# First batch fetched in halves of 48 rows, the sum of f put ahead of its rounded copy, and new offsets for the planner of a spectral and gated feed-forward kernel

## The chip, the core and the metric

The kernel runs on one core of a Trainium2 chip. The metric is the device time of one execution in microseconds (us). TensorE is called PE, VectorE DVE, ScalarE ACT, GpSimd POOL, and SyncE SP, which issues the DMAs; PEld is the load of weights into PE. About 0.2% of the time, 5.1 us, is what a measurement of this kernel can tell from no change.

## The reference, cut to what matters

```python
X = np.fft.rfft(x, axis=1)                      # x: 8 batches, 3008 tokens, 256 channels
Yr = Xr @ w_r - Xi @ w_i + b_r
Yi = Xr @ w_i + Xi @ w_r + b_i
Y  = sign(Y) * max(abs(Y) - 0.01, 0)            # each part by itself
y  = np.fft.irfft(Yr + 1j * Yi, n=3008, axis=1)
t  = y.reshape(24064, 256)
out = (silu(t @ w_gate) * (t @ w_val)) @ w_out  # 256 -> 1536 -> 256
```

## The kernel before, in words

There are two stages. The first, about the first 515 us, is the spectral one: the transform over 3008 = 47 x 64 tokens, the mixing of the channels, the shrinking and the transform back. The second, the remaining 2040 us, is the gated feed-forward part, 24 blocks of tokens by 6 pairs of hidden slices, in an order written out by hand. The change does not touch the second stage.

The first stage is made of named steps:

- `x_first k` (k = 0 to 7, first batch only) fetches 128 rows of 1024 numbers. In the prepared input, rows 0 to 46 and 64 to 110 hold tokens, row 47 and row 111 hold zeros, and the other 32 rows hold zeros that nothing reads: the products take rows 0 to 47 and 64 to 111. A row of this input stands 4352 bytes after the one before.
- `first k` is the product of that chunk with the small constant matrix `wa` (48 x 64 by 48 x 512, function `stage_a`) into two banks of PSUM. Two `turn` steps, transposes on DVE, then carry the banks to SBUF. For the later batches the same is done by `x k` and `tiles k`, each `x k` in one transfer of 128 rows.
- For each of 96 pairs (8 batches by 12): `second` (PE, from the turned chunks and the constants `wf`) writes `ps_b`. ACT copies one half of it to `f` (step `f`) and rounds the whole (step `f_hi`); DVE adds the other half to `f` (step `f_sum`) and takes the rest that rounding lost (`f_lo`); ACT and POOL or DVE do the same for the sum (`flat_hi`, `flat_lo`). `sum` (PE) multiplies the sum, `spread` (DVE) puts it with the bias into `mixb`, `mix` (PE) adds the two other products, and `gather`, `clip`, `shrink`, `y_hi`, `y_lo`, `back`, `z` and `store` follow. `ps_b` is one bank, so `second` of a pair waits for `f_lo` of the pair before.
- `z_in n` fetches, in two transfers of 48 rows each (rows 0 to 47, then rows 64 to 111, 4 KB a row), what `store` wrote to DRAM; two rows of one of these transfers lie 64 KB apart in DRAM.
- `load_seven` turns 18 weight matrices of 64-bit numbers into rounded halves, between the pairs.

The set-up also makes three rounded weight matrices: `wm 1` and `wm 2` (POOL) from `wj` and `wr`, then `wm_hi`, `negate`, `bias` (ACT) and `wm_lo` (POOL).

All steps are handed to a planner (class `Plan`). Each has a key, and the table `SHIFT` moves the keys of a kind of step; the planner simulates the engines with a fixed cost for each step and writes out one order for each engine, and an engine keeps that order. Where the planner sees PE idle in the first 40 us it puts in `idle` products, whose results nothing uses.

Before the planned order, POOL clears the tile `warm`, ACT loads a table with one activation on that tile, and PE multiplies `warm` by itself three times (L719 and L721).

Of the kernel before, what the change touches and what calls it, by code (L numbers as in the profile page):

```python
# [44 lines left out]
FEED = 84  # L45
SHIFT = {"add": -0.5, "lower": 0.5, "third": -0.5, "turn5": 0.12, "turn4": 0.06, "turn0": -0.44, "y_hi": -0.37, "f": -0.5, "out": 0.75, "spread": 0.0, "back": -0.19, "raw": 0.37, "second": 0.06, "y_lo": 0.68, "shrink": 0.44, "z_in": 0.06, "mix": 0.5, "wr": -1.0, "turn1": 0.0, "tiles": 0.56, "turn6": -0.31, "wo": 0.06, "x_sum": -0.5, "sum": -0.5, "flat_lo": -0.12, "xt1": 0.18, "x": 0.12, "store": 0.37, "turn": -0.32, "wm": -0.12, "bits down": -0.5, "upper": 0.25, "wj": -0.12, "kept": -1.0, "negate": 0.25, "turn3": 0.12, "unit": 0.56, "wm_hi": -0.12, "z": 0.5, "bias": -0.44, "wi_lo": -0.06, "turn2": -0.18, "x_hi": -0.5, "clip": -0.5, "xt0": -0.25, "wa": 0.06, "warm": 0.25, "bits up": -1.5}
# [4 lines left out]
WARM = 1  # L51
FULL = 40.0
# [223 lines left out]
def transform(ctx, tc, front, ring, last, ps_, feed, xp, w_r, w_i, cb, wup_raw, wdn_raw, ca, cf, ci, cq, w21, wup_d, wdn_d, xt_d, d2):  # L276
    nc = tc.nc
# [37 lines left out]
    def head(plan):  # L315
# [4 lines left out]
        def fetch_first(k):  # L320
            where = ("x_raw", "x_raw", "wo", "wo", "z_in", "z_in", "z_in", "w")[k]
            if where == "x_raw":
                box[k] = take()
            elif where == "w":
                box[k] = scratch[:, : 2 * T]
            elif where == "z_in":
                box[k] = last.tile([P, 2 * T], F32, name="x_first", tag=where, bufs=3)
            else:
                if k == 2:
                    box["wo"] = last.tile([P, 4 * T], F32, name="x_first", tag=where, bufs=1)  # L330
                box[k] = box["wo"][:, (k - 2) * 2 * T : (k - 1) * 2 * T]
# [800 lines left out]
```

## Time and profile before

| what | us |
|---|---|
| median of 3 runs (2557.44 to 2557.63) | 2557.52 |
| the profiled execution's own time | 2556.73 |
| its span, first to last instruction | 2554.9 |
| PE busy in the span | 2544.8 |
| DVE, POOL and ACT busy | 2064.7, 2082.1 and 1705.0 |

The 1.8 us between the span and the execution's own time lie around the program. "Busy" of PE is modelled, since products are pipelined. The page shows a granted clock of 90% or more in every slice. A row of the timeline has its start, its length, the engine, the line, the operation, and in brackets how long the engine was idle before it and what ended that; a DMA named there has landed just before.

### The profile page before, as it was taken

What the parts mean: (1) busy time and instruction counts of PE and PEld (TensorE: products, weight loads), DVE (VectorE), ACT (ScalarE), POOL (GpSimd) and SP (SyncE); (2) the same over time, 40 slices, a digit from 0 to 9 for tenths busy, and PEclk for the clock granted to TensorE, in tenths of its full rate; (3) what the DMA queues carried; (4) which work ended last, traced back from release to release, by engine and by line L of the source; (5) the groups of instructions that cost most, each with busy time, mean ns of one, the idle gap of its engine ahead of it and who ended that gap; (6) DMA issues with size and microseconds to landing.
All of it is one profiled execution on the core that took longest, in us unless ns stands there. A gap on an engine that the chain in (4) does not pass through costs nothing.

```text
span 2554.9 us, 45902 instructions
## 1 busy us (share of the span) xinstructions
PE 2544.8 (100%) x16534; PEld 2136.0 (84%) x16534; DVE 2064.7 (81%) x2998; ACT 1705.0 (67%) x3342; POOL 2082.1 (81%) x1595
## 2 busy tenths in 40 slices
PE   9999999999999999999999999999999999999999
PEld 6888888978888888888888888888888888888899
DVE  7989898677877877887788788878887888788887
ACT  6888888966666665666656666666666566656665
POOL 5777777568888888888888888888888888888886
PEclk9999999999999999999999999999999999999999
DMA  6788888855445444544444444444444444444453
GB/s 236 246 293 277 287 281 273 252 206 183 159 154 177 163 154 153 175 157 151 160 158 150 141 163 163 151 142 163 163 151 143 162 163 146 142 158 158 151 182 123
DMA packets 133924, 460.57 MB, mean 180 GB/s; under 512 B 13632, under 2 KB 58944, under 8 KB 133696
## 3 DMA queue, kind: packets, MB, share of 16 engines
q1 hardware_dynamic: 133552, 457.53, 54.0%
q8 instruction: 131, 2.15, 0.4%
q14 instruction: 97, 0.79, 0.1%
q10 hardware_dynamic: 144, 0.10, 0.0%
HBM read 366.61 MB, written 90.96 MB: 179 GB/s over the span
## 4 chain that ended last, share of the span: by engine, by line
PE 97%; DVE 1%; DMA 1%; ACT 0%; issue 0%; POOL 0%; SPq 0%; DVEq 0%
PE bank L791 79%; PE mixb L535 5%; PE ps_b L513 3%; PE ps_s L520 3%; PE ps_z L559 3%; PE ps_x L650 2%; PE ps_a L470 2%; PE bank L1037 0%; DMA x_first<-xp 0%; DMA scratch<-xp 0%; PE ps_z L557 0%; DVE y_lo L594 0%; ACT t L547 0%; DVE f_lo L578 0%; POOL t L586 0%
## 5 line engine op out<-in xcount | busy, mean ns | idle before, releaser
L791 PE MATMUL bank<-x_near,wup 128*128 128x512 f32 (+1 forms) x4032 | 1035.8, 386 | 0.4 <-DVE bank L964 0.2
L811 POOL TENSOR_TENSOR h_parts<-more,h_parts 128x512 fp32r<-128x512 f32 (+1 forms) x572 | 847.2, 1495 | 101.8 <-ACT h_parts L807 100.7
L791 PEld LDWEIGHTS bank<-x_near,wup 128*128 128x128 f32 x4032 | 751.0, 188 | 152.7 <-DVE bank L964 3.9
L791 PE MATMUL bank<-h_parts,wdn 128*128 128x512 f32 (+1 forms) x3024 | 835.3, 385 | 0.0
L811 POOL TENSOR_TENSOR h_parts<-hidden,h_parts 128x512 fp32r<-128x512 f32 (+1 forms) x431 | 563.7, 1319 | 213.7 <-ACT h_parts L807 176.9
L791 PEld LDWEIGHTS bank<-h_parts,wdn 128*128 128x128 f32 x3024 | 564.9, 188 | 108.5 <-POOL h_parts L811 0.3
L807 ACT CAST h_parts<-hidden 128x512 fp32r<-128x512 f32 (+1 forms) x433 | 265.5, 613 | 451.0 <-DVE hidden L937 449.7
L791 PE MATMUL bank<-x_parts,wup 128*128 128x512 f32 (+1 forms) x2016 | 525.7, 384 | 0.0
L937 DVE TENSOR_TENSOR hidden<-hidden,bank 128x512 f32<-128x512 f32 (+1 forms) x576 | 375.8, 674 | 78.1 <-PE bank L791 69.6
L791 PEld LDWEIGHTS bank<-x_parts,wup 128*128 128x128 f32 x2016 | 375.4, 188 | 71.7 <-DVE bank L964 1.7
L832 DVE TENSOR_TENSOR sums<-sums,bank 128x512 f32<-128x512 f32 (+1 forms) x357 | 240.2, 673 | 234.3 <-PE bank L791 234.3
L807 ACT CAST h_parts<-more 128x512 fp32r<-128x512 f32 (+1 forms) x572 | 349.3, 611 | 39.3 <-DVE more L802 28.4
L935 ACT ACTIVATE hidden<-bank 128x512 f32<-128x512 f32 (+1 forms) x432 | 252.6, 585 | 114.6 <-PE bank L791 113.9
L802 DVE TENSOR_TENSOR more<-hidden 128x512 f32<-128x512 f32 (+1 forms) x286 | 291.9, 1059 | 0.0
L802 DVE TENSOR_TENSOR more<-hidden,more 128x512 f32<-128x512 f32 (+1 forms) x286 | 257.7, 901 | 0.0
L942 ACT COPY bank<-bank 128x512 f32<-128x512 f32 (+1 forms) x288 | 161.6, 561 | 109.3 <-DVE hidden L937 103.9
L964 DVE TENSOR_TENSOR bank<-hidden,bank 128x512 f32<-128x512 f32 (+1 forms) x288 | 196.9, 684 | 36.3 <-PE bank L791 23.5
L586 POOL TENSOR_TENSOR t<-t,y 128x512 f32<-128x512 f32 x94 | 129.3, 1376 | 70.1 <-DVE y L585 63.1
L950 ACT COPY hidden<-bank 128x512 f32<-128x512 f32 (+1 forms) x288 | 167.6, 582 | 2.2
L547 ACT COPY t<-mixb 64x256 f32<-64x256 f32 x384 | 140.9, 367 | 22.0 <-PE mixb L535 17.1
L243 POOL TENSOR_TENSOR x_near<-xf,x_near 128x512 fp32r<-128x512 f32 (+1 forms) x112 | 142.3, 1286 | 5.2 <-PE bank L791 4.8
L986 DVE TENSOR_TENSOR hidden<-hidden,bank 128x512 f32<-128x512 f32 (+1 forms) x144 | 97.4, 676 | 42.7 <-PE bank L791 42.4
(111 smaller groups left out, 3104.1 us busy)
## 6 DMA issues: line engine op xcount, KB each, us to landing
wup<-wup_d SPq DMA_DIRECT2D x288, 896.0 KB, 4.7
scratch<-xp SPq DMA_DIRECT2D x59, 512.0 KB, 4.9
out<-o SPq DMA_DIRECT2D x88, 256.0 KB, 6.1
d<-z SPq DMA_DIRECT2D x84, 256.0 KB, 3.9
z_in<-d SPq DMA_DIRECT2D x112, 192.0 KB, 5.1
xt_d<-xt SPq DMA_DIRECT2D x56, 376.0 KB, 4.7
xf<-xt_d SPq DMA_DIRECT2D x15, 1024.0 KB, 7.8
wup_d<-wup SPq DMA_DIRECT2D x12, 896.0 KB, 5.8
```

Source lines behind the costliest of these rows:

```text
L243: low = lambda: eng.tensor_tensor(part[:, 1, :h], src, f32(part[:, 0, :h]), op=ALU.subtract)
L547: nc.scalar.copy(t()[64 * half : 64 * half + 64, k * C : (k + 1) * C], mixb[64 * k : 64 * k + 64, half * C : (half + 1) * C])
L791: nc.tensor.matmul(o, lhsT=weights[w], rhs=parts[x], start=start and i == 0, stop=stop and i == 2, skip_group_check=True)
L802: v.tensor_tensor(at(o, h), at(a, h), at(b, h), op=ALU.subtract)
L807: act.copy(pair[i][:, 0, :h], at(i, h))
L811: eng.tensor_tensor(pair[i][:, 1, :h], at(i, h), f32(pair[i][:, 0, :h]), op=ALU.subtract)
L832: v.tensor_tensor(o, o, spare[:, :h], op=ALU.add)
L935: act.activation(at(i, h), src, AF.Silu)
L937: v.tensor_tensor(at(i, h), at(i, h), src, op=ALU.mult)
L942: act.copy(b3[:, :h], b1[:, :h])
L950: act.copy(m5, b2[:, :h])
L964: v.tensor_tensor(b2[:, :h], m5, b3[:, :h], op=ALU.add)
```

## The change

1. `x_first k` becomes two transfers, rows 0 to 47 and rows 64 to 111, and the unread rows are not fetched. SP issues 16 transfers in place of 8.
2. `wa` has no transfer of its own. It stands in 64 more columns of the first chunk; POOL copies it to its place, and `first 0` reads it where it landed.
3. DVE, not POOL, clears `warm`, and the activation that loads the table has a tile of its own, so PE's first products no longer wait for ACT. They are two of 128 columns and one of 512; the second of 512 (`clear`) stands behind `first 7`.
4. `wr` and `wj` change places, and offsets move `wf 0` behind the other constants. `wm 1`, `wm 2` and the `wm_lo` may run on POOL or DVE.
5. After planning, `f_sum` is put ahead of `f_hi` in the program's order, by moving one of the two past steps of other engines, so that `f_sum` is not behind `f_hi` in what it waits for.
6. `SHIFT` has new numbers and 17 more kinds of step, `BIAS` (which engine a step takes) four new ones, and 24 single steps have a `NUDGE`.

```diff
-SHIFT = {"add": -0.5, "lower": 0.5, "third": -0.5, "turn5": 0.12, ...
+SHIFT = {"add": -0.5, "lower": 0.68, "third": -0.5, "turn5": 0.15, ...
-BIAS = {'y_lo POOL': 0.2, 'z DVE': 1.7, 'flat_lo DVE': 1.2, 'shrink DVE': 1.5}
+BIAS = {"y_lo POOL": 0.3, "z DVE": 0.7, "flat_lo DVE": 2.2, "shrink DVE": 0.8}
+NUDGE = {"shrink 33": -0.5, "flat_lo 17": -0.25, "tiles 41": 0.25, ...
-        key += SHIFT.get(name.split()[0], 0) * SLOT
+        key += (SHIFT.get(name.split()[0], 0) + NUDGE.get(name, 0)) * SLOT
+    HALVES = slice(0, 48), slice(64, 112)
-            nc.sync.dma_start(box[k], xp[0, k, :, : 2 * T])
+            wide = 2 * T if k else 2 * T + 64
+            if not k:
+                box[k] = scratch[:, 5 * T : 5 * T + wide]
+            for rows in HALVES:
+                nc.sync.dma_start(box[k][rows], xp[0, k, rows, :wide])
-        plan.add("wa", "SP", 0.45, -39.5, [], load_wa, 2.0)
+        plan.add("wa", "POOL", 0.2, -39.5, ["x_first 0"], lambda: [g.tensor_copy(wa[rows], box[0][rows, 2 * T :]) for rows in HALVES])
-        plan.add("wr", "SP", 0.45, -24, [], load("wr", ...
-        plan.add("wj", "SP", 0.45, -23, [], load("wj", ...
+        plan.add("wr", "SP", 0.45, -19.2, [], load("wr", ...
+        plan.add("wj", "SP", 0.45, -23.8, [], load("wj", ...
+        either = {"POOL": 1.23, "DVE": 0.61}
-        plan.add("wm_lo 0", "POOL", 1.23, 0.3 * SLOT, ["wm_hi 0"], lambda: lower(0))
+        plan.add("wm_lo 0", either, None, 0.3 * SLOT, ["wm_hi 0"], lambda eng: lower(0, eng), wide=True)
...
-    nc.gpsimd.memset(warm, 0.0)
-    nc.scalar.activation(warm[:, 0:1], warm[:, 0:1], AF.Silu)
-    for _ in range(WARM):
-        nc.tensor.matmul(mixed[0][:, :C], lhsT=warm[:, :P], rhs=warm[:, C:], start=True, stop=True)
-    for bank in mixed:
-        nc.tensor.matmul(bank, lhsT=warm[:, :P], rhs=warm, start=True, stop=True)
+    table = k1p.tile([P, 1], F32, name="table")
+    v.memset(warm, 0.0)
+    nc.gpsimd.memset(table, 0.0)
+    nc.scalar.activation(table, table, AF.Silu)
+    for _ in range(2):
+        clear(0, P)
+    clear(0)
+    plan.add("clear", "PE", 0.87, -1.0, ["turn 0 10", "turn 0 11"], lambda: clear(1))
     order = plan.order()
+    for j in range(B * NP):
+        names = [name for name, _ in order]
+        i, k = names.index(f"f_hi {j}"), names.index(f"f_sum {j}")
+        between = {engine for _, engine in order[i + 1 : k]}
+        if i < k and "ACT" not in between:
+            order.insert(k, order.pop(i))
+        elif names.index(f"f {j}") < i < k and "DVE" not in between:
+            order.insert(i, order.pop(k))
```

How the order moves, at three places. The first is SP's queue at the start of the program. Before (`scratch` and `x_first` are the eight chunks, `wa`, `wr`, `wj`, `wf`, `bias` and `raw_i` the constants):

```order
L332 DMA scratch<-xp 128x1024
L309 DMA wa<-ca 128x64
L332 DMA scratch<-xp 128x1024
L332 DMA x_first<-xp 128x1024 x5
L332 DMA scratch<-xp 128x1024
L350 DMA wr<-w_r 128x2x256
L313 DMA wf<-cf 128x768
L350 DMA bias<-bias 128x512
L350 DMA wj<-w_i 128x2x256
L350 DMA raw_i<-ci 128x256
```

And of the change:

```order
L335 DMA scratch<-xp 48x1088 x2
L335 DMA scratch<-xp 48x1024 x2
L335 DMA x_first<-xp 48x1024 x10
L335 DMA scratch<-xp 48x1024 x2
L353 DMA wj<-w_i 128x2x256
L353 DMA wr<-w_r 128x2x256
L353 DMA raw_i<-ci 128x256
L353 DMA bias<-bias 128x512
L312 DMA wf<-cf 128x768
```

The chunks are 16 transfers of 48 rows, `wa` is gone, and `wf` moved from the second of the constants to the last.

The second is ACT's order from its first step on the weights to the first rounded sum (`wm_hi` and `wsum` are the weights, `f` and `f_hi` of pair 0). Before:

```order
L372 CAST wm_hi<-wr 128x512
L383 ACTIVATE bias<-bias 32x256 x2
L576 COPY f<-ps_b 128x256
L575 CAST f_hi<-ps_b 128x4x2x64
L375 CAST wm_hi<-wsum 128x512
L579 CAST f_hi<-f 128x256
L384 CAST wi_hi<-raw_i 128x256
L377 ACTIVATE wsum<-wsum 128x512
L378 CAST wm_hi<-wsum 128x512
```

And of the change:

```order
L377 CAST wm_hi<-wr 128x512
L380 CAST wm_hi<-wsum 128x512
L388 ACTIVATE bias<-bias 32x256
L382 ACTIVATE wsum<-wsum 128x512
L383 CAST wm_hi<-wsum 128x512
L388 ACTIVATE bias<-bias 32x256
L389 CAST wi_hi<-raw_i 128x256
L582 COPY f<-ps_b 128x256
L581 CAST f_hi<-ps_b 128x4x2x64
L585 CAST f_hi<-f 128x256
```

All steps on the weights, the bias and `wi_hi` now stand ahead of the first `f`; before, four of them stood behind it.

The third is PE from its first product to the last of the eight `first` (`mixb` from `warm` are products whose results nothing uses, `ps_a` are the `first`). Before:

```order
L719 MATMUL mixb_130<-warm 128x256
L721 MATMUL mixb_130<-warm 128x512
L721 MATMUL mixb_131<-warm 128x512
L470 MATMUL ps_a<-scratch,wa 64x512 x8
L470 MATMUL ps_a<-x_first,wa 64x512 x20
L470 MATMUL ps_a<-scratch,wa 64x512 x4
```

And of the change:

```order
L727 MATMUL mixb_130<-warm 128x128 x2
L727 MATMUL mixb_130<-warm 128x512
L476 MATMUL ps_a<-scratch 64x512 x4
L476 MATMUL ps_a<-scratch,wa 64x512 x4
L476 MATMUL ps_a<-x_first,wa 64x512 x20
L476 MATMUL ps_a<-scratch,wa 64x512 x4
L727 MATMUL mixb_131<-warm 128x512
```

The products ahead of the first `ps_a` shrink from one of 256 and two of 512 columns to two of 128 and one of 512, and the other of 512 stands behind the last `first`.

## Rows read from the trace of the kernel before

**Rows 1.** The page: busy time of each engine; the chain that ended last.

```profile
PE 2544.8 (100%) x16534; PEld 2136.0 (84%) x16534; DVE 2064.7 (81%) x2998; ACT 1705.0 (67%) x3342; POOL 2082.1 (81%) x1595
...
PE 97%; DVE 1%; DMA 1%; ACT 0%; issue 0%; POOL 0%; SPq 0%; DVEq 0%
```

**Rows 2.** Windows: stretch, length, busy by engine, granted clock, DMA share, GB/s.

```profile
0.00:20.00 20.00, 16.25 (x116) 7.13 (x116) 10.66 (x18) 4.65 (x10) 4.17 (x8) 1.00 0.91 338
...
20.00:100.00 80.00, 78.28 (x587) 64.30 (x580) 70.77 (x124) 64.05 (x152) 55.80 (x53) 1.00 0.63 205
100.00:500.00 400.00, 399.76 (x6031) 351.52 (x6029) 342.88 (x562) 343.72 (x814) 306.06 (x276) 1.00 0.88 280
```

**Rows 3.** Timeline of PE in the first 26 us: start, length, work.

```profile
2.28 1.22 PE L719 MATMUL mixb<-warm 128*128 128x256 f32 x2 [2.28 <-ACT warm L717]
3.29 3.22 PE L721 MATMUL mixb<-warm 128*128 128x512 f32 x4
6.45 1.95 PE L470 MATMUL ps_a<-scratch,wa 48*64 48x512 f32 x16
...
14.78 1.09 PE L470 MATMUL ps_a<-scratch,wa 48*64 48x512 f32 x8 [0.25 <-DMA scratch<-xp]
...
16.46 0.71 PE L513 MATMUL ps_b<-wf,d 128*128 128x128 f32 x4 [0.15 <-DMA wf<-cf]
...
17.93 1.28 PE L742 MATMUL ps_x<-warm 128*128 128x128 f32 x10
...
20.47 1.21 PE L513 MATMUL ps_b<-wf,d 128*128 128x128 f32 x8
...
25.50 0.28 PE L535 MATMUL mixb<-wm_hi,f_hi 128*128 128x256 f32 x1
```

**Rows 4.** Windows of two stretches in which SP's loads fill the DMA engines.

```profile
5.00:13.00 8.00, 7.37 (x51) 1.77 (x49) 5.43 (x10) 0.00 (x0) 0.00 (x0) 1.00 1.02 402
...
474.00:478.00 4.00, 4.00 (x37) 4.00 (x36) 2.74 (x5) 3.98 (x10) 3.31 (x3) 1.00 1.03 221
```

**Rows 5.** Timeline of SP: DMA issues; the last covers six.

```profile
0.74 0.39 SPq L332 DMA_DIRECT2D scratch<-xp  x1
...
2.12 2.77 SPq L332 DMA_DIRECT2D x_first<-xp  x5
...
472.12 2.95 SPq L639 DMA_DIRECT2D z_in<-d  x6
```

**Rows 6.** DMA issue at 0.74 us: count, size, us from issue to landing.

```profile
scratch<-xp SPq DMA_DIRECT2D x1, 512.0 KB, 3.4
```

**Rows 7.** Timeline of ACT, from the first weights on.

```profile
15.36 0.62 ACT L372 CAST wm_hi<-wr 128x512 fp32r<-128x512 f32 x1 [13.13 <-DMA wr<-w_r]
17.03 0.84 ACT L383 ACTIVATE bias<-bias 32x256 f32<-32x256 f32 x2 [1.05 <-DMA bias<-bias]
18.13 0.37 ACT L576 COPY f<-ps_b 128x256 f32<-128x256 f32 x1 [0.25 <-PE ps_b L513]
18.40 0.59 ACT L575 CAST f_hi<-ps_b 128x512 fp32r<-128x512 f32 x1
...
19.67 0.40 ACT L579 CAST f_hi<-f 128x256 fp32r<-128x256 f32 x1
19.98 0.40 ACT L384 CAST wi_hi<-raw_i 128x256 fp32r<-128x256 f32 x1
20.38 0.63 ACT L377 ACTIVATE wsum<-wsum 128x512 f32<-128x512 f32 x1
```

**Rows 8.** Timeline of POOL and of DVE at the start.

```profile
17.84 2.51 POOL L364 TENSOR_TENSOR wsum<-wj,wr 128x512 f32<-128x512 f32 x2 [0.50 <-DMA wj<-w_i]
...
7.57 9.68 DVE L475 STREAM_TRANSPOSE d<-ps_a 128x512 f32<-128x512 f32 x16 [7.57 <-PE ps_a L470]
...
19.36 0.68 DVE L578 TENSOR_TENSOR f_lo<-ps_b,f_hi 128x512 fp32r<-128x512 f32 x1
```

**Rows 9.** Groups by line, 6 to 515 us: count, busy us, mean ns, idle before.

```profile
L594 DVE TENSOR_TENSOR y_lo<-t,y_hi 128x512 fp32r<-128x512 f32 x73 | 65.0, 890 | 4.2 <-ACT y_hi L587 3.8
...
L577 DVE TENSOR_TENSOR f<-f,ps_b 128x256 f32<-128x256 f32 x96 | 39.9, 416 | 37.4 <-ACT f_hi L575 30.3 <-issue 2.7 <-ACT f L576 1.7
```

More of the change, by code (lines that the diff above doesn't have):

```diff
@@ L45 @@
 FEED = 84
-SHIFT = {"add": -0.5, "lower": 0.5, "third": -0.5, "turn5": 0.12, "turn4": 0.06, "turn0": -0.44, "y_hi": -0.37, "f": -0.5, "out": 0.75, "spread": 0.0, "back": -0.19, "raw": 0.37, "second": 0.06, "y_lo": 0.68, "shrink": 0.44, "z_in": 0.06, "mix": 0.5, "wr": -1.0, "turn1": 0.0, "tiles": 0.56, "turn6": -0.31, "wo": 0.06, "x_sum": -0.5, "sum": -0.5, "flat_lo": -0.12, "xt1": 0.18, "x": 0.12, "store": 0.37, "turn": -0.32, "wm": -0.12, "bits down": -0.5, "upper": 0.25, "wj": -0.12, "kept": -1.0, "negate": 0.25, "turn3": 0.12, "unit": 0.56, "wm_hi": -0.12, "z": 0.5, "bias": -0.44, "wi_lo": -0.06, "turn2": -0.18, "x_hi": -0.5, "clip": -0.5, "xt0": -0.25, "wa": 0.06, "warm": 0.25, "bits up": -1.5}
+SHIFT = {"add": -0.5, "lower": 0.68, "third": -0.5, "turn5": 0.15, "turn4": 0.52, "turn0": 0.0, "y_hi": -0.12, "f": -0.3, "out": 1.5, "spread": 0.37, "back": 0.8, "raw": 0.68, "second": 0.06, "y_lo": 0.74, "shrink": -0.02, "z_in": 1.12, "mix": 0.57, "wr": -4.04, "turn1": -0.27, "tiles": 0.56, "turn6": 1.15, "wo": 1.57, "x_sum": -2.25, "sum": -0.2, "flat_lo": 0.44, "xt1": 1.37, "x": 1.75, "store": -0.92, "turn": -0.08, "wm": -0.04, "bits down": -0.5, "upper": 1.77, "wj": -3.5, "kept": 0.17, "negate": -0.72, "turn3": 0.34, "unit": 3.18, "wm_hi": -1.85, "z": 0.43, "bias": -0.08, "wi_lo": 1.45, "turn2": 0.29, "x_hi": 0.06, "clip": -1.05, "xt0": -0.5, "wa": 2.47, "warm": 1.44, "bits up": -1.5, "gather": 1.01, "wf": 0.59, "bits": -2.11, "raw_i": -0.35, "wm_lo": -3.08, "wi_hi": -0.06, "early": -2.13, "flat_hi": 0.38, "f_lo": 0.31, "clear": 3.06, "sums": -1.18, "f_hi": 0.04, "first": 2.42, "f_sum": 0.01, "xf": 4.57, "x_first": -2.26, "x_lo": -4.29}
 REACH = 160
 LOOSE = 95
-BIAS = {'y_lo POOL': 0.2, 'z DVE': 1.7, 'flat_lo DVE': 1.2, 'shrink DVE': 1.5}
+BIAS = {"y_lo POOL": 0.3, "z DVE": 0.7, "flat_lo DVE": 2.2, "shrink DVE": 0.8}
+NUDGE = {"shrink 33": -0.5, "flat_lo 17": -0.25, "tiles 41": 0.25, "f_sum 67": -0.25, "xt0 8": 0.5, "bits up 10": 0.25, "gather 42": 0.25, "f 54": 0.25, "out 8": -0.25, "turn4 up 7": 0.25, "back 80": -0.5, "z_in 21": -0.25, "turn2 up 4": 0.5, "turn4 up 9": -0.25, "z_in 49": -0.25, "back 52": 0.25, "mix 40": -0.5, "f 88": -0.5, "xt0 23": -0.25, "mix 73": -0.25, "turn 6 14": -0.25, "kept up 6": 0.5, "flat_hi 39": -0.25, "shrink 60": 0.5}
 SLOT = 5.5
-WARM = 1
 FULL = 40.0
@@ L249, in spectral_ffn @@
 @with_exitstack
-def spectral_ffn(ctx: ExitStack, tc: tile.TileContext, xp, w_r, w_i, cb, wup_raw, wdn_raw, ca, cf, ci, cq, out):
+def spectral_ffn(ctx: ExitStack, tc: tile.TileContext, xp, w_r, w_i, cb, wup_raw, wdn_raw, cf, ci, cq, out):
     nc = tc.nc
@@ L268, in spectral_ffn @@
         with ExitStack() as one:
-            finish, stored = transform(one, tc, front, ring, last, ps_, feed, xp, w_r, w_i, cb, wup_raw, wdn_raw, ca, cf, ci, cq, w21, wup_d, wdn_d, xt_d, d2)
+            finish, stored = transform(one, tc, front, ring, last, ps_, feed, xp, w_r, w_i, cb, wup_raw, wdn_raw, cf, ci, cq, w21, wup_d, wdn_d, xt_d, d2)
         finish()
@@ L273, in spectral_ffn, with transform @@
     next(ffn, None)
-def transform(ctx, tc, front, ring, last, ps_, feed, xp, w_r, w_i, cb, wup_raw, wdn_raw, ca, cf, ci, cq, w21, wup_d, wdn_d, xt_d, d2):
+def transform(ctx, tc, front, ring, last, ps_, feed, xp, w_r, w_i, cb, wup_raw, wdn_raw, cf, ci, cq, w21, wup_d, wdn_d, xt_d, d2):
     nc = tc.nc
@@ L292, in transform @@
     stored = []
-    places = [scratch[:, i * T : (i + 2) * T] for i in (3, 5)]
+    places = [scratch[:, i * T : (i + 2) * T] for i in (5, 3)]
     def take():
@@ L355, in head @@
         plan.add("wf 0", "SP", 0.45, -25, [], lambda: load_wf(0), 2.0, moves=384 * MOVE)
-        plan.add("wr", "SP", 0.45, -24, [], load("wr", [P, 2, C], "t", half_w(w_r), bufs=2), 2.0, moves=256 * MOVE)
-        plan.add("wj", "SP", 0.45, -23, [], load("wj", [P, 2, C], "t", half_w(w_i), bufs=2), 2.0, moves=256 * MOVE)
+        plan.add("wr", "SP", 0.45, -19.2, [], load("wr", [P, 2, C], "t", half_w(w_r), bufs=2), 2.0, moves=256 * MOVE)
+        plan.add("wj", "SP", 0.45, -23.8, [], load("wj", [P, 2, C], "t", half_w(w_i), bufs=2), 2.0, moves=256 * MOVE)
         plan.add("bias", "SP", 0.45, -22, ["warm"], load("bias", [P, 2, C], "bias", cb), 2.0, moves=256 * MOVE)
@@ L361, in combine, with fn, lower @@
         def combine(i, op):
-            def fn():
+            def fn(eng):
                 box["w", i] = sb.tile([P, 2, C], F32, name="wsum", tag="z")
-                g.tensor_tensor(box["w", i], box["wj"], box["wr"], op=op)
+                eng.tensor_tensor(box["w", i], box["wj"], box["wr"], op=op)
             return fn
-        def lower(i):
+        either = {"POOL": 1.23, "DVE": 0.61}
+        def lower(i, eng):
             src = box["w", i] if i else box["wr"]
-            g.tensor_tensor(wmix[i][1], src, f32(wmix[i][0]), op=ALU.subtract)
+            eng.tensor_tensor(wmix[i][1], src, f32(wmix[i][0]), op=ALU.subtract)
         plan.add("wm_hi 0", "ACT", 0.51, -20, ["wr"], lambda: nc.scalar.copy(wmix[0][0], box["wr"]))
-        plan.add("wm_lo 0", "POOL", 1.23, 0.3 * SLOT, ["wm_hi 0"], lambda: lower(0))
-        plan.add("wm 1", "POOL", 1.23, 0.5 * SLOT, ["wj"], combine(1, ALU.subtract))
+        plan.add("wm_lo 0", either, None, 0.3 * SLOT, ["wm_hi 0"], lambda eng: lower(0, eng), wide=True)
+        plan.add("wm 1", either, None, 0.5 * SLOT, ["wj"], combine(1, ALU.subtract), wide=True)
         plan.add("wm_hi 1", "ACT", 0.51, 0.7 * SLOT, ["wm 1"], lambda: nc.scalar.copy(wmix[1][0], box["w", 1]))
-        plan.add("wm 2", "POOL", 1.23, 0.6 * SLOT, ["wj"], combine(2, ALU.add))
+        plan.add("wm 2", either, None, 0.6 * SLOT, ["wj"], combine(2, ALU.add), wide=True)
         plan.add("negate", "ACT", 0.51, 0.8 * SLOT, ["wm 2"], lambda: nc.scalar.mul(box["w", 2], box["w", 2], -1.0))
         plan.add("wm_hi 2", "ACT", 0.51, 0.9 * SLOT, ["negate"], lambda: nc.scalar.copy(wmix[2][0], box["w", 2]))
-        plan.add("wm_lo 2", "POOL", 1.23, 1.1 * SLOT, ["wm_hi 2"], lambda: lower(2))
-        plan.add("wm_lo 1", "POOL", 1.23, 1.0 * SLOT, ["wm_hi 1"], lambda: lower(1))
+        plan.add("wm_lo 2", either, None, 1.1 * SLOT, ["wm_hi 2"], lambda eng: lower(2, eng), wide=True)
+        plan.add("wm_lo 1", either, None, 1.0 * SLOT, ["wm_hi 1"], lambda eng: lower(1, eng), wide=True)
         for q in (1, 3):
@@ L389, in head @@
             "spread 0": ["bias 1", "bias 3"],
+            "spread 1": ["clear"],
             "mix 0": ["wm_lo 1", "wm_lo 2"],
@@ L463, in fetch, with stage_a @@
         nc.sync.dma_start(t, xp[b, k, :, : 2 * T])
-    def stage_a(tags, xt):
+    def stage_a(tags, xt, wa=wa):
         banks = [ps_.tile([P, T], F32, name="ps_a", tag=tag) for tag in tags]
@@ L715, in transform, with clear @@
     warm = k1p.tile([P, T], F32, name="warm")
-    nc.gpsimd.memset(warm, 0.0)
-    nc.scalar.activation(warm[:, 0:1], warm[:, 0:1], AF.Silu)
-    for _ in range(WARM):
-        nc.tensor.matmul(mixed[0][:, :C], lhsT=warm[:, :P], rhs=warm[:, C:], start=True, stop=True)
-    for bank in mixed:
-        nc.tensor.matmul(bank, lhsT=warm[:, :P], rhs=warm, start=True, stop=True)
+    table = k1p.tile([P, 1], F32, name="table")
+    v.memset(warm, 0.0)
+    nc.gpsimd.memset(table, 0.0)
+    nc.scalar.activation(table, table, AF.Silu)
+    def clear(bank, cols=T):
+        nc.tensor.matmul(mixed[bank][:, :cols], lhsT=warm[:, :P], rhs=warm[:, :cols], start=True, stop=True)
+    for _ in range(2):
+        clear(0, P)
+    clear(0)
+    plan.add("clear", "PE", 0.87, -1.0, ["turn 0 10", "turn 0 11"], lambda: clear(1))
     plan.add("warm", "ACT", 0.2, -50, [], lambda: None)
@@ L737, in idle @@
             for half in range(2):
-                rows = slice(64 * half, 64 * half + 48)
+                rows = slice(0, 48)
                 for g in range(2):
-                    nc.tensor.matmul(mixed[half][64 * g : 64 * g + 64, :P], lhsT=wa[rows], rhs=warm[rows, :P], start=False, stop=True, skip_group_check=True)
+                    nc.tensor.matmul(bank[64 * g : 64 * g + 64, half * P : half * P + P], lhsT=wa[rows], rhs=warm[rows, :P], start=False, stop=True, skip_group_check=True)
         else:
@@ L1106 @@
     k = fourier_constants()
+    xp = xp.reshape(B, NCH // 2, P, 2 * T + 64)
+    xp[0, 0, :, 2 * T :] = k["wa"]
     arrays = {
```

10 lines of the change are left out of this document (3 added, 7 removed).

## The prediction

> **What bounds the kernel now.** I read the page first: PE is busy for 2544.8 of 2554.9 us, and 97% of the chain that ended last is PE [rows 1]. So only time in which PE stands idle, or works on nothing, can be won, and whatever delays PE's first real work is lost in full. The windows say where: PE is idle for 3.75 us of the first 20, 1.72 us between 20 and 100, and 0.24 us between 100 and 500 [rows 2]. The change touches nothing after that. The rest of the edge is hidden in PE's timeline [rows 3]: up to 6.45 us it multiplies the cleared tile, the last chunk of the first batch lands just before 14.78, `wf` just before 16.46, at 17.93 it runs unused products again, and the first `mix`, from which on work is always waiting, begins at 25.50. That start of `mix` is the one number to follow; PE's order from `second 0` to there keeps the same real steps.
>
> **First products.** PE's first product waits until 2.28 us for ACT, and the three unused ones keep it until 6.45 [rows 3], while the first chunk, issued at 0.74, landed 3.4 us later, at 4.1 [rows 5, 6]. In the change DVE clears the tile, ACT is out of the way, and half of the columns or more are gone: two of 128 and one of 512, 768 columns, in place of 1280, which took 4.17 us together. At the same pace that is 2.5 us; starting near 1.2 they end near 3.7, so `first 0` waits for its chunk, near 4.1, and is 2.3 us earlier. What it buys depends on the chunks behind it.
>
> **The chunks, the term that decides.** The eight chunks fall from 4.19 to 3.15 MB. What they gain depends on the rate of transfers of 48 rows. The chunks of 128 rows ran at 402 GB/s with the DMA engines full (share 1.02) [rows 4]. The only transfers in this trace of the new shape, 48 rows of 4 KB, first into the rows from 0 and then into those from 64, are those of `z_in`; six of them were issued from 472.12 on [rows 5], and while they filled the engines (share 1.03) they moved 221 GB/s [rows 4]. That is 55% of the rate, with the engines just as busy, so 75% of the bytes take 136% of the time. The two ends are therefore 3.15/0.402 = 7.8 us and 3.15/0.221 = 14.3 us; I take 221, the row of the same shape, queue and alternation, and keep 402 as a rival, since `z_in` also reads another place in DRAM.
>
> [...]
>
> The last chunk: the first has 0.74 us until its issue and 3.4 us to landing, of which 512 KB at 402 GB/s are 1.3; so start and landing are 2.85 us. Then 2.85 + 14.35 = 17.2 us, against 14.78 before (where the 10.5 us of transfer also had `wa` in their midst). That is 2.4 us later. Sixteen issues at the pace of five in 2.77 us [rows 5] take 8.9 us and are not the limit.
>
> **The constants.** They follow the chunks in the queue, and their spacing is read from what they released: `wr` 0.6 us after the last chunk, `wf` 1.1, `bias` 0.6, `wj` 0.8 [rows 3, 7, 8]; `raw_i` is half of `wj`, 0.4. In the new order `wj` lands at 18.0, `wr` 18.6, `raw_i` 19.0, `bias` 19.6 and `wf` 20.7 (before 16.46). POOL then makes `wm 1` and `wm 2` in 2.51 us [rows 8], to 21.1. ACT has, all ahead of the first `f` now, `negate` 0.63 (21.7), `wm_hi` 0.62 (22.4), half of `bias` 0.42 (22.8), `wi_hi` 0.40 (23.2) [rows 7]. So `f` of pair 0 begins at 23.2 and not at 18.13: 5.1 us late. `second 0` is done by 22, behind `wf`, and does not decide.
>
> **The sum of f ahead.** DVE's `f_sum` stood idle for 30.3 us in all, released by ACT's `f_hi` [rows 9]; before, `f` ended at 18.50, `f_hi` at 18.99, and the rounding of the sum began at 19.67 [rows 7]. Beside `f_hi` it costs nothing and saves up to 0.59 us, the length of `f_hi`, in each pair's chain. In pair 0: `f_hi` ends at 24.1, `f_lo` (0.68 [rows 8]) waits for `f_sum` and one transpose (9.68/16 = 0.60 [rows 8]) and ends at 25.3, so `second 1` begins at 25.35 against 20.47 [rows 3]: 4.9 late. From there to `mix` 5.03 us went by; one more `f_sum` in that chain gives back 0.4. `mix` begins near 30.0, 4.5 us late. From 100 us on PE has 0.24 us of idle time to give, so the same edit in the other 90 pairs is worth nothing there, however long DVE waited.
>
> **Offsets, biases, nudges.** They reorder steps in the rest of the stage. The most that they can win is the idle time from 20 to 100 us, less what belongs to the head, and 0.24 behind it: some 1.9 us. The most they could lose, if 100 to 500 became as ragged as 20 to 100 (1.72 in 80 us), is 400/80 x 1.72 - 0.24 = 8.4 us. I take -0.5, near the row of 100 to 500, where there is nothing to win. The program has 88 of the 96 `y_lo` on DVE, 14 more: 14 x 0.89 = 12.5 us [rows 9], beside PE, since DVE is busy for 343 of 400 us in the long stretch [rows 2]; if that cover went, each would lengthen a pair's chain by some tenths. POOL's two copies of `wa` lie beside `first 0`, which reads the landed chunk.
>
> **Sum.** +4.5 - 0.5 = +4.0 us. The profiled execution took 2556.73 (its span and 1.8 us around it): 2560.7. It lies 0.8 below the median of the runs, 2557.52, so the time predicted is 2561.5.
>
> **Rivals.**
>
> *The halves run at the full rate.* For it: the slow `z_in` reads rows 64 KB apart, `xp` has its rows 4352 bytes apart. Against it: in the window of `z_in` the DMA engines are as busy, and nothing shows which side holds them. Then the last chunk lands near 2.85 + 7.8 = 10.7; DVE, with 16 transposes from about 5.5 us, ends at 15.2 (17.25 before [rows 8]); `wr` lands at 12.1, POOL is done at 14.6, ACT at 16.7, and `f` begins 1.4 us early, `mix` 2.0: 2557.52 - 2.0 - 0.5 = 2555.0 (the issues, 8.9 us long, may take back 0.7). It decides from the rate: at about 290 GB/s (last chunk near 13.7, `f` 1.6 late, `mix` 1.0 late) the time is 2558.0, no change; above 305 GB/s it is faster than before.
> [...]
>
> [...]
>
> *The new order stalls PE in the long stretch.* Half of the bound above, 4.2 us: 2565.7 with slow halves. For it: the offsets and 24 nudges touch a stretch that has only 0.24 us to win. Against: the planner still gives each step the same needs.
>
> **Chances.** Slow halves, as forecast: 0.52, own range 2559.5 to 2563.5. A rate between the two ends (2557 to 2559): 0.12. Full rate: 0.22. Lower clock: 0.08. Stalls: 0.06. 0.2%, 5.1 us, is about what a measurement of this kernel can tell from no change; the bounds are 2552.4 and 2562.6. Faster: the best third of the full rate, 0.07. Slower: the two last, 0.14, and a fifth of the forecast, 0.11: 0.25. Same: 0.68. The range, 2554.5 to 2563.8, leaves out the lower half of the faster cases and most of the two last.
>
> **What would show it.** Right: in the first 18 us a DMA share near 1.0 at some 220 GB/s; the last `first` near 17; `wf` behind it; `f` of pair 0 released by ACT's own queue, not by PE; the first `mix` near 30. Wrong: 400 GB/s there, and `mix` before 25. The step on `f_sum` is right when its idle time behind `f_hi` is gone. The offsets are misjudged if PE's idle time between 100 and 500 us grows beyond 1 us. [...]

## The result, and the profile after

The changed kernel took 2585.55 us (median of 5 runs, 2581.7 to 2586.64) against 2557.52 of the kernel before in the same comparison: 28 us more, a ratio of 1.0107, 95% interval [1.0093, 1.0122]. The forecast was 2561.5, with a range up to 2563.8. The profiled execution took 2585.5 us, with a span of 2583.7.

The page of the changed kernel, busy time and the chain that ended last, for [rows 1]:

```profile
PE 2560.9 (99%) x16524; PEld 2140.9 (83%) x16524; DVE 2064.2 (80%) x3016; ACT 1700.3 (66%) x3341; POOL 2050.0 (79%) x1581
...
PE 87%; DVE 6%; ACT 4%; issue 2%; POOL 1%; DMA 0%; DVEq 0%; ACTq 0%; POOLq 0%
```

PE's share of the chain fell from 97 to 87%, and DVE and ACT have 10% between them. The windows of the changed kernel, with the columns of [rows 2], say where:

```profile
0.00:20.00 20.00, 18.55 (x70) 6.36 (x70) 10.54 (x16) 1.49 (x2) 0.77 (x7) 1.00 0.94 197
5.00:13.00 8.00, 8.00 (x38) 2.49 (x35) 4.94 (x8) 0.00 (x0) 0.23 (x1) 1.00 1.03 199
20.00:100.00 80.00, 75.39 (x538) 59.18 (x535) 64.15 (x113) 56.61 (x134) 45.14 (x44) 1.00 0.54 184
100.00:500.00 400.00, 390.64 (x5593) 338.47 (x5592) 334.91 (x568) 326.34 (x780) 273.28 (x257) 1.00 0.85 270
```

PE stands idle for 4.6 us from 20 to 100 and for 9.4 us from 100 to 500, where 1.72 and 0.24 were idle before [rows 2]. More is lost than that: in the long stretch it did 5593 instructions and not 6031, with 69.8 ns of busy time for each and not 66.3; in part that is because the stretch now holds an earlier piece of the work. The start of each pair's `mix` on PE follows the delay (us from the span's start, each from PE's timeline):

| `mix` of pair | before | after | later by |
|---|---|---|---|
| 0 | 25.5 | 32.6 | 7.1 |
| 15 | 94.9 | 107.2 | 12.3 |
| 45 | 255.1 | 272.9 | 17.9 |
| 95 | 512.4 | 541.3 | 28.9 |

So 7 us are lost ahead of the first `mix`, and 22 more over the 95 pairs behind it: 0.35 us a pair up to pair 15, some 0.2 from there on. The head first, in PE's timeline of the changed kernel, for [rows 3]:

```profile
1.45 2.93 PE L727 MATMUL mixb<-warm 128*128 128x128 f32 x6 [1.45 <-DVE warm L723]
4.31 2.59 PE L476 MATMUL ps_a<-scratch 48*64 48x512 f32 x8
...
17.89 3.02 PE L476 MATMUL ps_a<-scratch,wa 48*64 48x512 f32 x8
20.83 2.07 PE L727 MATMUL mixb<-warm 128*128 128x512 f32 x2
...
23.13 0.92 PE L519 MATMUL ps_b<-wf,d 128*128 128x128 f32 x4
...
24.32 0.64 PE L519 MATMUL ps_b<-wf,d 128*128 128x128 f32 x4
...
27.36 1.21 PE L519 MATMUL ps_b<-wf,d 128*128 128x128 f32 x8
...
30.82 1.21 PE L519 MATMUL ps_b<-wf,d 128*128 128x128 f32 x8 [0.53 <-DVE f_lo L584]
...
32.58 0.28 PE L541 MATMUL mixb<-wm_hi,f_hi 128*128 128x256 f32 x1
```

The first `first` begins 2.1 us earlier, the last one 3.1 us later, and `second 1`, at 27.36, 6.9 us later. ACT's timeline of the changed kernel, for [rows 7]:

```profile
20.18 0.62 ACT L377 CAST wm_hi<-wr 128x512 fp32r<-128x512 f32 x1 [17.95 <-DMA wr<-w_r]
...
24.59 0.41 ACT L389 CAST wi_hi<-raw_i 128x256 fp32r<-128x256 f32 x1
25.00 0.37 ACT L582 COPY f<-ps_b 128x256 f32<-128x256 f32 x1
25.86 0.59 ACT L581 CAST f_hi<-ps_b 128x512 fp32r<-128x512 f32 x1 [0.49 <-DVE f L583]
```

`f` has no releaser but ACT's own queue: it stands behind `wi_hi`, as forecast. But it is a tie: `second 0` ended at 24.96, and 0.04 us is also the lag by which `f` follows it in n1, n10 and n13 (below), where PE does release it. The last row is new: `f_hi` waits for DVE's `f_sum`. The groups by line of the changed kernel (6 to 545 us), for [rows 9], show that this is so in most pairs (ACT idles before 87 of the 96 `f_hi`):

```profile
L584 DVE TENSOR_TENSOR f_lo<-ps_b,f_hi 128x512 fp32r<-128x512 f32 x96 | 66.2, 690 | 55.0 <-ACT f_hi L581 54.9
L581 ACT CAST f_hi<-ps_b 128x512 fp32r<-128x512 f32 x96 | 56.4, 588 | 59.3 <-DVE f L583 59.1
L583 DVE TENSOR_TENSOR f<-f,ps_b 128x256 f32<-128x256 f32 x96 | 39.6, 412 | 14.8 <-ACT f L582 13.8 <-ACT f_hi L581 0.9
```

`f_sum`'s wait for `f_hi` (30.3 us [rows 9]) is gone, as the change says. In its place `f_hi` waits 59.1 us for `f_sum`, and then `f_lo` 54.9 us for `f_hi`. One pair of the long stretch, before and after, shows the hand-overs (timelines of ACT and DVE together). Before:

```profile
127.35 0.38 ACT L576 COPY f<-ps_b 128x256 f32<-128x256 f32 x1 [0.35 <-PE ps_b L513]
127.62 0.59 ACT L575 CAST f_hi<-ps_b 128x512 fp32r<-128x512 f32 x1
128.24 0.42 DVE L577 TENSOR_TENSOR f<-f,ps_b 128x256 f32<-128x256 f32 x1
128.58 0.68 DVE L578 TENSOR_TENSOR f_lo<-ps_b,f_hi 128x512 fp32r<-128x512 f32 x1
```

And after:

```profile
132.90 0.37 ACT L582 COPY f<-ps_b 128x256 f32<-128x256 f32 x1
133.80 0.41 DVE L583 TENSOR_TENSOR f<-f,ps_b 128x256 f32<-128x256 f32 x1
134.24 0.59 ACT L581 CAST f_hi<-ps_b 128x512 fp32r<-128x512 f32 x1 [0.45 <-DVE f L583]
134.87 0.69 DVE L584 TENSOR_TENSOR f_lo<-ps_b,f_hi 128x512 fp32r<-128x512 f32 x1 [0.66 <-ACT f_hi L581]
```

Before, the work passes from ACT to DVE once; after, it goes ACT, DVE, ACT, DVE, and both stand idle in turn, ACT for 0.45 us and DVE for 0.66 in this pair. `f_lo` ends 4.22 us after the start of `second` (median of 96 pairs), 3.57 before. The next `second` needs `f_lo`.

### The profile page after: what moved, and what is told of

It is laid out like the page before. It is cut to its first block, busy times and chain, and to the rows that moved or that the text cites. A ratio compares the mean times of both kernels' runs of the same rounds, so it can differ in the third digit from the quotient of the medians.

```text
span 2583.7 us, 45908 instructions
## 1 busy us (share of the span) xinstructions
PE 2560.9 (99%) x16524; PEld 2140.9 (83%) x16524; DVE 2064.2 (80%) x3016; ACT 1700.3 (66%) x3341; POOL 2050.0 (79%) x1581
## 4 chain that ended last, share of the span: by engine, by line
PE 87%; DVE 6%; ACT 4%; issue 2%; POOL 1%; DMA 0%; DVEq 0%; ACTq 0%; POOLq 0%
PE bank L810 78%; PE mixb L541 2%; PE ps_b L519 2%; PE ps_a L476 1%; PE ps_z L565 1%; ACT t L553 1%; DVE d L481 1%; PE ps_s L526 1%; ACT f_hi L581 1%; DVE f_lo L584 1%; DVE y_lo L600 1%; PE ps_x L656 1%; DVE f L583 1%; ACT z L604 1%; DVE mixb L530 1%
```

## Experiments

Medians in one table; each ratio is to the kernel before, run beside it on the same chip.

| run | us | ratio, 95% interval |
|---|---|---|
| n1_no_swap | 2565.76 | 1.0034 [1.0022, 1.0047] |
| n2_before_swap | 2581.25 | 1.0093 [1.0078, 1.0109] |
| n3_whole_rows | 2580.66 | 1.0090 [1.0075, 1.0105] |
| n4_no_swap_whole | 2561.93 | 1.0017 [1.0007, 1.0026] |
| n6_old_tables_no_swap_whole | 2570.77 | 1.0058 [1.0041, 1.0075] |
| n7_r112 | 2564.82 | 1.0028 [1.0016, 1.0039] |
| n8_cols | 2562.19 | 1.0018 [1.0008, 1.0028] |
| n10_sum_off_psum | 2584.53 | 1.0105 [1.0090, 1.0120] |
| n12_no_swap_sum_off_psum | 2585.41 | 1.0109 [1.0095, 1.0123] |
| n13_hi_off_psum | 2559.60 | 1.0008 [0.9999, 1.0017] |
| n14_old_head_keys | 2559.99 | 1.0013 [1.0004, 1.0022] |
| c1_before_new_head | 2555.84 | 0.9996 [0.9987, 1.0005] |

**The swap of `f_sum` and `f_hi`, out of the change and alone in the kernel before.** n1 leaves the loop out, n2 adds it to the kernel before:

```diff
-    for j in range(B * NP):
...
-            order.insert(i, order.pop(k))
```

> The changed kernel without the step that puts f_sum ahead of f_hi; all else as changed. Theory S (f_hi now waits for f_sum and f_lo for f_hi, two more hand-overs of the bank ps_b for each pair, and PE waits for f_lo): most of the 21.8 us lost after the first mix comes back, 2563 to 2568 us, PE idle below 3 us between 100 and 500, the first mix still near 32. Theory T (the new offsets, biases and nudges order the stretch badly by themselves): 2578 to 2585 us.

> The kernel before with the one step that puts f_sum ahead of f_hi. Theory S: 2570 to 2580 us, ACT idle before f_hi behind f_sum some 50 us in the first stage. Theory T: 2556 to 2560 us.

Without it the change takes 19.8 us less; the kernel before takes 23.6 us more with it, 1.3 us beyond the range expected of n2. In n1 the delay of `mix` is 7.3 us at pair 0 and still 6.7 at pair 75; in n2 it is 1.4 and grows to 24.1. The windows of n1 and n2 in the long stretch:

```profile
100.00:500.00 400.00, 397.10 (x5908) 349.67 (x5905) 338.80 (x579) 341.71 (x811) 290.43 (x266) 1.00 0.88 281
```

```profile
100.00:500.00 400.00, 389.00 (x5619) 336.60 (x5621) 333.01 (x546) 326.01 (x776) 293.51 (x269) 1.00 0.83 269
```

PE works 6.5 us more without the loop in the one, and 10.8 us less with it in the other [rows 2]. PE, DVE, ACT and POOL keep their orders (in n2 two neighbours on ACT trade places); what the loop changes is which of the two steps stands first in the program.

**Why the swap costs: one bank.** Both steps read all partitions of the PSUM bank `ps_b`. n13 keeps the swap and takes `f_hi` off the bank; `f_lo`, the bank less `f_hi`, takes up the difference, which the text on record overlooks:

```diff
-  lambda: nc.scalar.copy(first(f_hi()), both()))
+  lambda: nc.scalar.copy(first(f_hi()), bias[0]...))
```

> The changed kernel, swap kept, but f_hi casts the 128x512 of bias (SBUF, not written any more by then) in place of the bank ps_b, so f_hi is wrong and the output is not the reference's; f_sum and f_lo stay as they are. ACT's operation keeps its shape, and f_hi no longer touches the bank that f_sum reads. Theory S (f_hi stands behind f_sum only because both read one bank): f_hi follows f at once, its idle of 59.1 us behind f_sum goes, f_lo's end falls from 4.2 to 3.6 or 3.7 us after second's start, and the time to 2561 to 2568 us. Rival O (the order itself, whatever f_hi reads): 2583 to 2587 us.

2559.6 us: 26 us are gone, more than the swap costs and 1.4 us below the range of theory S; `f_lo` ends 3.77 us after the start of `second`. The same lines in n13's groups, and one pair of it:

```profile
L581 ACT CAST f_hi<-bias 128x512 fp32r<-128x512 f32 x96 | 60.7, 632 | 0.0
L583 DVE TENSOR_TENSOR f<-f,ps_b 128x256 f32<-128x256 f32 x96 | 39.7, 414 | 18.1 <-ACT f L582 17.8
```

```profile
120.59 0.38 ACT L582 COPY f<-ps_b 128x256 f32<-128x256 f32 x1
120.86 0.63 ACT L581 CAST f_hi<-bias 128x512 fp32r<-128x512 f32 x1
121.00 0.42 DVE L583 TENSOR_TENSOR f<-f,ps_b 128x256 f32<-128x256 f32 x1
121.52 0.69 DVE L584 TENSOR_TENSOR f_lo<-ps_b,f_hi 128x512 fp32r<-128x512 f32 x1
```

Here `f_hi` and `f_sum` run at the same time (in this pair for 0.42 us), which the prediction took for granted. In n1 `f_sum` still waits 45.3 us for `f_hi`; here neither waits for the other, and n13 lies 2.6 us above the kernel before, n1 8.1. Not one of the 96 `f_hi` waits, and the program has no wait for DVE on any of them, where the changed kernel has one on 91, and the kernel before on 13, in which `f_sum` stood first already. One of them in each:

```
L581 CAST f_hi<-ps_b 128x4x2x64 [waits DVE_49]     changed kernel
L575 CAST f_hi<-ps_b 128x4x2x64                    before
L581 CAST f_hi<-bias 128x4x2x64                    n13
```

Whichever of the two stands later in the program waits: `f_sum` in the kernel before (30.3 us [rows 9]), `f_hi` in the changed one (59.1). In n13, where only one of them reads the bank, neither does. The wait is there; what would happen without it, no run here shows.

n10 tried the same from the other side, `f_sum` off the bank with the swap kept; it adds `f` to itself. n12 is the same without the swap:

```diff
-  v.tensor_tensor(blocks(total()), blocks(total()), both()[:, :, 1], op=ALU.add)
+  v.tensor_tensor(blocks(total()), blocks(total()), blocks(total()), op=ALU.add)
```

> The changed kernel with f_sum still ahead of f_hi, but its second operand read from f itself (SBUF) in place of the second half of the bank ps_b, so the sum is twice f and not f plus the other half, and the output is not the reference's. Same count of instructions, same shapes, same order on every engine. Theory S (f_hi stands behind f_sum because both read the one PSUM bank): f_hi then follows f at once on ACT, its idle behind f_sum (59.1 us in 87 instances in the changed kernel) falls under 10 us, PE's wait of second for f_lo goes back to some 1 us in a few instances, and the time to 2561 to 2567 us, about that of the version without the swap (2565.8). Rival O (the place in the order alone, or f_sum's own time ahead of f_lo on DVE, costs it): nothing changes, 2583 to 2587 us.

> The control to n10: f_sum again adds f to itself from SBUF (output not the reference's), and the swap is taken out as well. In n10 the wait of f_hi was gone, but the add itself took 0.88 us in the mean where it took 0.41 from the bank, 45 us more of DVE, so its time tells nothing of the swap by itself. Theory S (the swap acts only through the shared bank, and n10's time is the slower add): with or without the swap the same, 2581.5 to 2587.5 us, f_lo's end 4.2 to 4.3 us after second's start as in n10. Rival O (the order costs some 20 us by itself): 2563 to 2569 us.

n10 missed: the time stayed. Its groups say why:

```profile
L583 DVE TENSOR_TENSOR f<-f 128x256 f32<-128x256 f32 x96 | 84.5, 880 | 14.0 <-ACT f L582 13.8
...
L581 ACT CAST f_hi<-ps_b 128x512 fp32r<-128x512 f32 x96 | 57.8, 602 | 0.0
```

`f_hi` no longer waits, but the add takes 880 ns and not 412, 45 us more of DVE in the stage, and `f_lo` ends 4.25 us after `second` begins, as late as with the wait. By itself that run could not part the two theories. The control does: with the add off the bank, the swap makes no difference that can be told (2584.53 with it, 2585.41 without), where it costs 19.8 us with the add on the bank.

**The chunks.** n3 and n4 fetch each chunk in one transfer of 128 rows, n3 with the swap and n4 without. n7 fetches rows 0 to 111 in one, n8 all rows in two transfers of half of the columns; both are without the swap:

```diff
-            for rows in HALVES:
-                nc.sync.dma_start(box[k][rows], xp[0, k, rows, :wide])
+            nc.sync.dma_start(box[k], xp[0, k, :, :wide])
```

> The changed kernel with each of the eight chunks in one transfer of 128 rows instead of two of 48; the order of all engines is the same. Theory P (transfers of 48 rows run at half the rate): the first 20 us show some 380 GB/s, the first mix begins 6 to 8 us earlier, near 25, and the time is 2577 to 2580 us. If the order of the constants behind the chunks were the cause of the late start, the first mix stays beyond 29 and the time at 2582 to 2585 us.

> Both: f_sum stays behind f_hi and the chunks come whole. Theories S and P add up: 2555 to 2560 us. Theory T: 2571 to 2578 us.

> The changed kernel without the swap, each chunk in one transfer of rows 0 to 111 (the 16 rows of zeros between the halves included) in place of two of 48 rows. Theory R (a transfer of 48 rows keeps half of the rate, 0.98 us each; one of 112 rows runs near 400 GB/s, 1.1 to 1.2 us for a chunk against 1.28 of 128 rows): the last chunk lands near 13, the first mix at 27 to 28 us, 2560 to 2562. Rival B (rows that are no whole 128 run at the lower rate): about 2.2 us for a chunk, last one past 20 us, 2568 or more.

> The changed kernel without the swap, each chunk in two transfers of all 128 rows and half of the columns each (2 KB a row) in place of two of 48 rows (4 KB a row). Theory R (the rows span sets the rate): each half lands in about 0.65 to 0.7 us after the one ahead, 350 to 400 GB/s in the first 15 us, 2561 to 2564. Rival N (two transfers for one, twice the issues and half of the bytes each, set it): about 200 to 270 GB/s and a last chunk at 17 us or later, 2565 to 2569.

Whole rows give back 4.9 us with the swap and 3.8 without, less than expected: the first `mix` begins at 28.3 (n3) and 28.2 (n4), not near 25, and the times lie 0.7 and 1.9 us above their ranges. The windows of n4, n7 and n8, in this order, while chunks fill the DMA engines:

```profile
5.00:13.00 8.00, 6.53 (x48) 1.36 (x40) 6.46 (x11) 0.00 (x0) 0.00 (x0) 1.00 1.02 400
```

```profile
5.00:13.00 8.00, 5.51 (x44) 1.21 (x45) 5.73 (x9) 0.00 (x0) 0.47 (x2) 1.00 1.02 289
```

```profile
5.00:13.00 8.00, 8.00 (x49) 2.06 (x42) 6.37 (x10) 0.00 (x0) 0.00 (x0) 1.00 1.03 372
```

The DMA engines are as busy in all (share 1.02 or 1.03): 400 GB/s with 128 rows, 372 with 128 rows in twice as many transfers of half the size, 289 with 112 rows, 199 with 48. So the number of transfers is not the cause, and neither is the source, which is `xp` in all four; the rate goes with the rows that a transfer spans. What makes it so, the rates do not show. n7 lies between its two theories: dropping the 16 rows of zeros saves an eighth of the bytes and loses more than a quarter of the rate (289 against 400 GB/s).

**What is left: constants, tables, head.** n6 is n4 with the old tables; n14 is n4 with the new tables but the old keys of the constants and the weight steps; c1 is the kernel before with only the edits of the head (`wa` inside chunk 0 in one transfer of 128 rows, DVE's clearing, a tile of its own for the table, one warm product less):

```diff
n6   -SHIFT (new), BIAS (new), NUDGE         +SHIFT, BIAS of the kernel before
n14  -plan.add("wr", ..., -19.2, ...         +plan.add("wr", ..., -24, ...     (and wj, wf 0, wm, bias, wi)
c1   -nc.gpsimd.memset(warm, 0.0)            +v.memset(warm, 0.0)              (and wa, table, WARM)
```

> The changed kernel without the swap, with each chunk in one transfer of 128 rows, and with the offsets, costs and (no) nudges of the kernel before, which also puts wf first among the constants. What is left of the change is the head: wa inside chunk 0, the DVE's memset, the shorter warm-up, weight steps free for DVE or POOL. The same with the new tables took 2561.9. Theory T (the new tables cost the 4.3 us that are left over the kernel before, 2.7 of them by the order of constants and of ACT's steps in the head): 2555.5 to 2558.5, the first mix at 25 to 26.5 us. Rival H (the head's other edits cost them): 2560 to 2563, the first mix near 28.

> The changed kernel without the swap, each chunk in one transfer of 128 rows (2561.9 us), with the new tables, but the keys of the constants' loads and of the weight steps put back to those of the kernel before: wr, wf, bias, wj, raw_i come in that order, and f of the first pair stands ahead of wm_hi 2 and negate on ACT. Theory K (the order of constants costs 2.7 us at the first mix, and these stay to the end): first mix at 25 to 26 us, 2558 to 2560 us. Rival L (a late head is caught up, the 4.3 us come from the order in the long stretch): first mix at 25 to 26 us, but 2561 to 2563.

> The kernel before with its tables, its planner's order and its constants, and only these edits of the head: wa comes inside chunk 0 in one transfer of 128 rows and is copied by POOL, DVE clears warm, a tile of its own for the activation table, one warm product less. Theory T (these edits gain up to the 0.9 us that n6 showed at the first mix; n6's later loss of 10 us is the old tables' order planned anew around a changed head): first mix at 24.6 to 25.3 us, 2556.6 to 2557.4 us. Rival H (the edits themselves disturb the long stretch): 2560 us or more.

n6 missed: its first `mix` is the earliest of all, at 24.6, yet it ends 13 us behind the kernel before, since its delay grows to 9.9 us at pair 95. Offsets fitted to one head lose about 9 us around another (2570.77 against n4's 2561.93); which step it is was not followed up. n14's first `mix` begins at 27.2, not at 25 to 26, because the new product `clear` and `wm_hi 1` stand ahead of the first `f`; it lies 3.0 us above the kernel before, n4 4.3, and their intervals overlap; in the traces its first `mix` is 0.9 us earlier (28.2 in n4). c1 begins its first `mix` at 25.0, 0.5 early, is 0.8 early up to pair 92 and 0.7 late from pair 93 on, and can't be told from the kernel before; its trace is that of the longest of its 11 runs (2557.54). Its median, 0.8 us below the range expected, is the fastest seen, and no version was shown to be faster than the kernel before.

## Why the prediction was wrong, step by step

**The sum of f ahead: this step failed.** "Beside `f_hi` it costs nothing and saves up to 0.59 us" put the two steps beside each other on two engines, and "the same edit in the other 90 pairs is worth nothing there". They read one bank and, before and after, run side by side in none of the 96 pairs: in the changed kernel `f_hi` waits 59.1 us for `f_sum`, and `f_lo` 54.9 us for `f_hi`. The row that told it was on the table: `f_sum` stood idle for `f_hi`, though it uses nothing that `f_hi` makes [rows 9]. I read that wait as the cost of a place in the order, and not as the sign of a shared resource that would make the other step wait once the order is turned. It cost 19.8 us of the 28.0 (n1), 23.6 alone (n2). Nor was a true side by side worth nothing in the other pairs: n13, where it happens, makes up 2.9 us of its delay from pair 0 to pair 95, and n1 loses 1.8.

**The chunks: right, size a little off.** Slow halves and a full DMA share (1.03) came as forecast, at 199 GB/s in place of 221. The same loads ran at 203 (n13), 212 (n10), 216 (n1) and 231 GB/s (n12) from 5 to 13 us, so 221 lies inside their scatter. The last half was issued at 10.85 and landed 7.9 us later, at 18.8, in place of 17.2:

```profile
scratch<-xp SPq DMA_DIRECT2D x1, 192.0 KB, 7.9
```

The rival of the full rate is out: `xp` has close rows and, at 199 to 231 GB/s, is as slow as `z_in` at 221 [rows 4].

**The constants: right, and late with the chunks.** `wr` released ACT at 20.18 (18.6 forecast), and `f` began at 25.00 behind ACT's own queue (23.2). `second 0` was to be done by 22 and ended at 24.96. `second 1` began at 27.36 (25.35), 2.0 late: 1.6 of the chunks, 0.2 of the steps on ACT, 0.2 of a transpose that waited 0.19 us for PE ahead of `f_lo`. `mix` began at 32.6 (30.0), 7.1 us later than before and not 4.5; the 0.6 us more is pair 1, where `f_lo` waits 0.65 us for `f_hi`, and `f_hi` for `f_sum`. In pair 0 that wait cost nothing: `f_hi` ended at 26.45, and `f_lo` began behind the transpose at 26.65. n1, without the swap, ends 8.1 us above the kernel before: that is what slow halves, constants and tables cost together, with 0.9 in which `f` waited for PE at the lower clock, where +4.0 was the sum. Whole rows take 3.8 of it; the old keys of the constants may take 1.3 more, which the intervals of n4 and n14 do not show.

**First products: right and without effect.** They ended at 4.38 (3.7 forecast), and `first 0` began at 4.31, 2.1 us earlier; the chunks behind it ate that. Of the 1280 columns 512 were gone, two fifths and not half; the forecast's 2.5 us go by the right 768.

**Offsets and nudges: small, the sign not shown.** n14, with the new tables but not the constants' keys, lies 3.0 us above the kernel before (0.04 to 0.22%): 1.7 at the first `mix`, and 1.2 more by pair 95, inside the bounds of -1.9 and +8.4 but not at -0.5. At pair 90 it is only 1.0 late, and c1, with the old tables, also loses 1.5 us between pairs 92 and 93, so the 1.2 can't be put down to the tables. PE is idle for 1.8 us of 100 to 500 there, against 0.24: beyond the 1 us that was to be the sign of misjudged offsets.

**Rivals.** Stalls in the long stretch did come, with a chance of 0.06 and a price of 4.2 us, of which the measured is five times; what made them was the swap, which I had not put into that rival. The lower clock, with a chance of 0.08, came too: in the changed kernel the two passes of 512 columns at 20.83 took 1.0 us each, and four of 128 at 23.13 took 0.92 us, against 0.64 at 24.32, as four took at 17.45 in the kernel before. But it ended at 23.8, ahead of `second 1` at 27.36, and `f` waited for ACT until 25.00 as well, so here it cost next to nothing. That it lasts to the first `mix`, no run shows; what n10 against n12 shows is 0.7 us there (below). In n1, n10 and n13 ACT stood idle ahead of `f` for 0.92, 0.67 and 0.71 us, waiting for `second 0`.

## What to carry to other kernels

Where an engine's step waits for a step of another engine whose result it doesn't use, look for what both touch, in this kernel one PSUM bank; here an edit that only turned the order moved the wait to the other engine (30.3 us on DVE before, 59.1 on ACT after), and what counted is how often the chain changes engines, not which wait went away. A wait that is gone proves nothing before the waits of its neighbours are read. And for a transfer that fills the DMA engines, leaving out rows can cost more rate than it saves bytes: here 75% of the bytes went at 199 GB/s in place of 402.

## What the hardware did that I had not expected

A DVE add of 128x256 with both inputs in SBUF took 880 ns in the mean in n10 (376 to 2341) and 872 in n12, beside a busy POOL (286.8 us of the 400 from 100 to 500 in n10), where the same add with one input in PSUM took 412 in the changed kernel. In n10, 54 of the 96 took over 500 ns, and 51 of these ended 0.28 us after the POOL operation that was running when they began; the 8 that met no POOL operation took at most 426 ns. So 51 of the 54 long ones go with a POOL operation beside them; why, the runs do not show.

The clock came up late in the changed kernel. In the kernel before, the trace has rows of the granted clock from 6.0 us on; ahead of that PE's passes of 512 columns began 0.85 us apart, which is 0.21 for 128 columns, where those of 128 at 17.93 began 0.11 us apart, though the windows read 1.00 where there is no row. In the changed kernel the rows begin at 23.8 us, and in n10, with the same head, at 24.4; up to there the passes are slow (in the changed kernel those of 128 columns began 0.21 us apart just ahead of 23.8, and 0.11 behind it). n1 and n13 had the full clock (1.00) from about 5 us on and half of it (0.50) from about 12 to 25, after PE had worked without a break from 1.45 us on; n12 had the full clock from 10.0 on with the same work. n4, where PE has gaps between the chunks, kept it; n3 and n14, which have such gaps too, had half of it from 8.8 to 15.6 and from 8.3 to 11.7. What decides it stays open. Windows of n13 and then of n4, at a clock of 0.50 and of 1.00:

```profile
16.00:20.00 4.00, 4.00 (x18) 0.95 (x12) 2.98 (x5) 0.15 (x1) 0.01 (x1) 0.50 1.07 259
```

```profile
16.00:20.00 4.00, 2.85 (x24) 1.99 (x22) 2.13 (x4) 2.92 (x6) 4.00 (x3) 1.00 0.92 363
```

n10 and n12 show the price at the first `mix`, since every engine has the same order in both. n12's begins 2.0 us earlier, at 29.9. Its loads account for 1.3 of that (`wr` released ACT at 18.06, and at 19.34 in n10), the clock for 0.7: `f` waited for PE in n10 and not in n12. ACT's row of the first `f` in n10 and then in n12:

```profile
24.82 0.37 ACT L582 COPY f<-ps_b 128x256 f32<-128x256 f32 x1 [0.67 <-PE ps_b L519]
```

```profile
22.78 0.36 ACT L582 COPY f<-ps_b 128x256 f32<-128x256 f32 x1
```
